# A delta-rule attention with two feed-forward layers: the first group's triangular inverses made in 16x16 blocks and joined on TensorE

## The chip, the cores and the metric

The kernel runs on one core of a Trainium2 chip. Its time is device microseconds of one execution. Three runs of the kernel before gave 926.7, 926.9 and 919.13 us (median 926.7). Engines: PE is TensorE, DVE is VectorE, ACT is ScalarE, POOL is GpSimd, SP is SyncE, whose queue issues every DMA of this kernel in one order.

## The reference

Four batches with eight heads, 768 positions and a head size of 48 go through a delta rule with a state S per head; the result, 3072 tokens of 384 features, goes through two feed-forward layers:

```python
k_n = k / (norm(k) + 1e-6)
for t in range(768):
    y[t] = q[t] @ S
    S = S + beta[t] * outer(k_n[t], v[t] - k_n[t] @ S)
x = y as [3072, 384]
h = x @ w_in;  solu = h * softmax(h);  x = layer_norm(solu) * g_ln @ w_out   # 384 -> 1024 -> 384
g = relu(x @ w2_in) ** 2;  out = g @ w2_out                                  # 384 -> 2048 -> 384
```

The weights arrive as float64, as pairs of 32-bit words.

## The kernel before, in words

**Chunks.** The recurrence is done in chunks of 64 tokens. A step is one chunk of one batch with all eight heads: 4 batches by 12 chunks are 48 steps, and two steps are a tile, 24 tiles in all. Inside a chunk the recurrence needs the inverse of a unit lower triangular 64x64 matrix I + L, with L the lower part of diag(beta) K K^T diag(1/norms). A step multiplies that inverse into the values (zstep, matmul line L1098, result z), then the chain uses z with the state (L1139 to L1182). Steps of one batch follow one another; a step's chain cannot start before its z.

**Inverses.** They are made for groups of tiles: group 0 is tiles 0 to 3, group 1 tiles 4 to 6, group 2 tiles 7 to 10, and four more. For a tile, e_tile multiplies K with K and with Q on PE (L684) out of operands that DVE spreads out by head first (L663), masks the products on DVE (L718), and sends the K K^T part to memory (gscr). norms and gammas work out 1/norm and beta/norm^2 per token in many ops of 24 or 32 elements on DVE. inversion reads gscr back as 32x32 blocks, one in each partition for many blocks at once (tile it), scales them (L881), does a forward substitution in 30 column steps of a multiply (L900) and an add (L917), each of which is split in two on the large steps, and scales again (L942). For group 0 this is on DVE, for groups 1 to 6 on POOL. ACT makes a transposed copy (ia, L959). Both go to memory (tscr, uscr); prep reads them back for one tile (tbd, t2) and joins two 32x32 blocks to a 64x64 one with two sets of 32x32 matmuls on PE (mm1 L1037, mm2 L1050) and copies on ACT (L1057, L1068).

**After that.** moe1_front (18 matmuls of 512 columns, L1218), moe1_back, and moe1_out (72 matmuls for a pair of tiles, L1340) do the first layer, beside the later steps of the recurrence. The second layer (L1483 and L1527) starts when the first has ended. load_w brings a weight piece in: the raw words by DMA into one of two buffers, an Abs on ACT, four DVE ops on 512 or 384 elements, then a high half (a cast on ACT) and a low half (a subtraction, split, L433); for the first layer's 14 pieces the low half is on POOL.

**What sets the order.** Every operation is recorded with an engine, a cost, a priority and what it reads and writes. A planner (class Plan) lays them out in a list schedule by those costs, in twelve rounds, and the kernel is then issued in that order by hand, so each engine and SP's queue run their instructions in a fixed order. The table of priorities (PR) is the same before and after.

## Time and profile before

| | |
|---|---|
| median of the runs | 926.7 us |
| profiled execution: span | 924.3 us (the page gives no other time of this execution) |
| instructions | 23182 |
| PE busy | 862.9 us, 93% of the span |
| DVE, ACT, POOL busy | 515.9, 487.0, 359.7 us |
| first z of tile 0 | at 72.46 us |
| first z of tile 4 (the first of group 1) | at 144.08 us |
| first z of tile 7 (the first of group 2) | at 206.95 us |
| second layer | from 504 us to the end |

Times in a row are microseconds from the start of the span. "PEld" is the loading of weights into PE. A line like L900 is a line of the kernel before; the release in square brackets names what ended an engine's idle time. PEclk is the granted clock of TensorE as a part of its full 2.4 GHz, averaged over the stretch. Rows of SP show the time in which its queue issues, not the transfer.

### The profile page before, as it was taken

The numbers are of one execution on the slowest core, as the hardware profiler recorded it, in microseconds if no ns is written. First come the engines' busy times: TensorE is split into PE (matmuls) and PEld (weight loads), VectorE is DVE, ScalarE is ACT, GpSimd is POOL, SyncE is SP. The second block draws the span as 40 slices with busy tenths as digits, with TensorE's granted clock in tenths as the row PEclk, the third lists the DMA queues.
The fourth block names the chain that finished last, engine by engine and source line by source line (L and its number), as shares of the span: only waits on it lengthen the run. The fifth ranks groups of instructions, "written<-read, shape, count | busy, mean of one in ns | idle before, by whom it ended". The sixth has DMA issues, their size and how long they took to land.

```text
span 924.3 us, 23182 instructions
## 1 busy us (share of the span) xinstructions
PE 862.9 (93%) x9144; PEld 806.9 (87%) x9144; DVE 515.9 (56%) x1063; ACT 487.0 (53%) x1069; POOL 359.7 (39%) x898
## 2 busy tenths in 40 slices
PE   6448888999999999999999999999999999999998
PEld 6447767988887888888788999999999999999998
DVE  6996777623877686766645655343333434343332
ACT  5336689766767667556565645343333434343333
POOL 6399889995468868998300000000000000000000
PEclk8565799999998999999899999999999999999999
DMA  8826967634778676463604432010010101000000
GB/s 238 207 99 157 246 185 210 157 109 113 200 241 251 176 224 179 139 195 114 190 24 144 127 98 77 10 43 10 1 52 1 52 1 52 1 26 1 27 1 26
DMA packets 129244, 101.75 MB, mean 110 GB/s; under 512 B 84080, under 2 KB 106608, under 8 KB 129136
## 3 DMA queue, kind: packets, MB, share of 16 engines
q1 hardware_dynamic: 129136, 100.28, 38.0%
q8 instruction: 72, 1.18, 0.5%
q14 instruction: 36, 0.29, 0.1%
HBM read 70.88 MB, written 29.36 MB: 108 GB/s over the span
## 4 chain that ended last, share of the span: by engine, by line
PE 75%; DVE 8%; DMA 6%; ACT 4%; POOL 3%; issue 2%; SPq 2%; ACTq 0%; DVEq 0%
PE acc L1527 22%; PE h L1483 22%; PE p_h L1218 9%; PE p_x L1340 9%; PE p_z L1098 3%; DMA kqe<-in_kine_dram 2%; PE p_tr L1320 2%; PE p_ep L684 2%; DVE itmp L900 2%; SPq L300 2%; DVE it L917 1%; PE p_a L1139 1%; PE p_o L1155 1%; POOL itmp L900 1%; POOL it L917 1%
## 5 line engine op out<-in xcount | busy, mean ns | idle before, releaser
L1504 DVE TENSOR_TENSOR xt<-xt 128x384 f32<-128x384 f32 x128 | 71.5, 558 | 165.3 <-ACT xt L1496 165.1
L1496 ACT ACTIVATE xt<-h 128x384 f32<-128x384 f32 x128 | 63.0, 492 | 170.7 <-PE h L1483 168.9
L1483 PE MATMUL h<-x1h,w2h 128*128 128x384 f32 x384 | 128.7, 335 | 0.0
L1483 PE MATMUL h<-x1l,w2h 128*128 128x384 f32 x384 | 128.6, 335 | 0.0
L1483 PE MATMUL h<-x1h,w2l 128*128 128x384 f32 x384 | 128.3, 334 | 0.0
L917 POOL TENSOR_TENSOR it<-it,itmp 128x72 f32<-128x72 f32 (+37 forms) x255 | 109.6, 444 | 5.2
L900 POOL TENSOR_TENSOR itmp<-it 128x72 f32<-128x72 f32 (+37 forms) x255 | 107.4, 436 | 2.2
L1340 PE MATMUL p_x<-zh,wgh 128*128 128x256 f32 x288 | 86.9, 302 | 1.3 <-ACT xo L1354 1.1
L1527 PE MATMUL acc<-woh,xl 128*128 128x384 f32 x258 | 87.4, 339 | 0.0
L1527 PE MATMUL acc<-wol,xh 128*128 128x384 f32 x258 | 87.3, 338 | 0.0
L1527 PE MATMUL acc<-woh,xh 128*128 128x384 f32 x258 | 87.0, 337 | 0.0
L1340 PE MATMUL p_x<-zl,wgh 128*128 128x256 f32 x288 | 81.7, 284 | 0.0
L1340 PE MATMUL p_x<-zh,wgl 128*128 128x256 f32 x288 | 81.5, 283 | 0.0
L433 DVE TENSOR_TENSOR xl<-xt,xh 128x384 fp32r<-128x384 f32 x86 | 48.0, 558 | 43.4 <-ACT xh L428 42.9
L1483 PEld LDWEIGHTS h<-x1h,w2l 128*128 128x128 f32 x384 | 72.1, 188 | 0.0
L1483 PEld LDWEIGHTS h<-x1h,w2h 128*128 128x128 f32 x384 | 72.1, 188 | 0.0
L1483 PEld LDWEIGHTS h<-x1l,w2h 128*128 128x128 f32 x384 | 72.1, 188 | 0.0
L428 ACT CAST xh<-xt 128x384 fp32r<-128x384 f32 x86 | 44.2, 514 | 46.1 <-DVE xt L1504 44.8
L1218 PE MATMUL p_h<-w1h,xh 128*128 128x512 f32 x144 | 65.4, 454 | 3.1 <-DVE ez L1251 3.1
L1098 PE MATMUL p_z<-m,tbd 128*128 128x112 f32 x384 | 58.1, 298 | 2.6 <-ACT zs L1109 1.4
L1218 PE MATMUL p_h<-w1h,xl 128*128 128x512 f32 x144 | 59.9, 416 | 0.2 <-DVE xl L433 0.2
L1218 PE MATMUL p_h<-w1l,xh 128*128 128x512 f32 x144 | 59.8, 415 | 0.0
(197 smaller groups left out, 2143.3 us busy)
## 6 DMA issues: line engine op xcount, KB each, us to landing
kql<-in_kin_dram SPq DMA_DIRECT2D x24, 512.0 KB
kqe<-in_kine_dram SPq DMA_DIRECT2D x40, 192.0 KB
raw<-in_w2i_dram SPq DMA_DIRECT2D x12, 512.0 KB
raw<-in_w2o_dram SPq DMA_DIRECT2D x16, 384.0 KB
gscr<-g SPq DMA_DIRECT2D x21, 256.0 KB
m<-in_ktok_dram SPq DMA_DIRECT2D x24, 192.0 KB
vt<-in_vtok_dram SPq DMA_DIRECT2D x24, 192.0 KB
x1scr<-xo SPq DMA_DIRECT2D x12, 384.0 KB
```

The costliest lines, as they stand in the source:

```text
L300: return add("sp", 0.06, lambda: nc.sync.dma_start(dst(), src()), r, w, prio, size, gate)
L428: add("act", c_act(n), lambda: act.copy(hi(), src()), r, [w[0]], prio)
L433: lambda: le.tensor_tensor(out=lo(), in0=src(), in1=hi().bitcast(F32), op=ALU.subtract),
L900: lambda tm=tm, j=j, nr=nr, w_=w_, c0=c0, c1=c1: eng.tensor_tensor(out=tm, in0=it[:, j + 1 :, j : j + 1].to_broadcast([P, nr, w_]), in1=it ...
L917: lambda tm=tm, j=j, c0=c0, c1=c1: eng.tensor_tensor(out=it[:, j + 1 :, c0:c1], in0=it[:, j + 1 :, c0:c1], in1=tm, op=ALU.add,),
L1098: pe.matmul(zp[:, p].rearrange("q (j c) -> q j c", j=7), tb[:, i * NP + p], m[:, i, :, p], start=True, stop=True,)
L1218: pe.matmul(p_h[:, sl], xx[:, c], ww[:, c, sl], start=(c == 0 and k == 0), stop=(c == 2 and k == 2),)
L1340: pe.matmul(p_x1[:, 0 : 2 * P], ww[:, f, c * P : c * P + P], zz[:, f], start=(f == 0 and k == 0), stop=(f == 7 and k == 2),)
L1483: pe.matmul(late["h2", ih], late[ww][:, c, s], xx[:, c], start=(c == 0 and k == 0), stop=(c == 2 and k == 2),)
L1496: lambda: act.activation(out=rt, in_=late["h2", ih], func=AF.Relu),
L1504: lambda: v.tensor_tensor(out=gg, in0=rt, in1=rt, op=ALU.mult),
L1527: pe.matmul(late["acc", a], gg[:, a * P : a * P + P], late[ww][:, f], start=(f == 0 and k == 0), stop=(f == 15 and k == 2),)
```

## The change

It makes group 0's inverses in another way and changes what stands around them.

- **first_group** (new) loads the keys of tiles 0 to 3 ahead of all else, in eight halves of 96 KB, and multiplies 32x32 blocks of K K^T on PE straight into one bank pair (p_h, 128 matmuls). DVE transposes the 32x32 squares of that (1024 elements a partition); each partition then has one row of every block, and the norms are on the diagonal. The scale factors take 17 DVE ops. The substitution runs in 16x16 blocks, two in a partition: 14 steps of a multiply and an add, of at most 112 elements. A scaling and two more transposes give the inverses of the diagonal blocks (d0) and their transposes (u0).
- **combine** (new) joins 16 to 32 (mma, mmb) and 32 to 64 (mm1, mm2) for each of tiles 0 to 3 on PE, 112 matmuls of 32 or fewer columns a tile, with copies on ACT and DVE between; **prep_first** (new) places the results in tbd, by ACT and DVE copies for tile 0 and by six DMAs inside SBUF for tiles 1 to 3. Group 0 no longer uses gscr, tscr and uscr.
- The products with Q of tiles 0 to 3 (**qk_first**) come later, from their own load. The values of a step are scaled on POOL.
- e_tile for tiles 4 to 9 multiplies 64-row operands straight from the loaded keys (eight matmuls of 128 columns for a step, where it was four of 96 rows) without the DVE ops that spread them by head. Their masks are all on DVE, the squares of norms on ACT.
- The first layer's weights: the pieces 3 and 4 use two more raw buffers, their first two DVE ops have one tensor input in place of two, and the 14 subtractions for the low halves go from POOL to DVE. All six w_in pieces are loaded in one go.
- Group 1's inverse on POOL uses another buffer for its products. gammas transposes on DVE in place of PE and ACT. The 20 warming matmuls are gone. The work for tiles 10 to 12 is issued two tiles later.

The core of the diff, in the order of the file:

```diff
-    raw, wu = raw_[i][:, 0:n], w.bitcast(U32)
+    raws, wu = raw_[i], w.bitcast(U32)
+    if n_w[0] in (3, 4):
+        x, kr = ((iaw[:, 0 : HB * HB], [("A", "ia")]), (ez_[0], [("ez", 0)]))[i]
+        raws = x.rearrange("q (n t) -> q n t", t=2).bitcast(U32)
+    raw = raws[:, 0:n]
...
+    if alone:
+        fns = (
+            lambda: v.tensor_scalar(out=w, in0=w, scalar1=F64_LO, scalar2=F64_HI, op0=ALU.max, op1=ALU.min),
+            lambda: v.tensor_scalar(
+                out=wu,
+                in0=wu,
+                scalar1=3,
+                scalar2=0x3FFFFFF8,
+                op0=ALU.logical_shift_left,
+                op1=ALU.bitwise_and,
+            ),
+        )
...
+    for i, fn in enumerate(fns):
+        add("dve", c_dve(n, alone), fn, [], [kw], prio, after=() if i else [*first_inv, *w2_gate])
...
 def load_w1i(i0, i1, prio):
     for i in range(i0, i1):
-        c, n = divmod(i, 2)
+        n, c = divmod(i, 3)
         s = slice(n * 512, n * 512 + 512)
-        w, kw = load_w(w1i[c, :, s], 512, prio)
+        w, kw = load_w(w1i[c, :, s], 512, prio, True)
         split(
             lambda c=c, s=s: w1h[:, c, s],
             lambda c=c, s=s: w1l[:, c, s],
...
-            "pool",
...
+            )[st % 4]
+            gp = bank.rearrange("q (p c) -> q p c", p=NP)
+            kq = kqe_[st % 3].rearrange("q p c -> q (p c)").rearrange("q (a p c) -> q a p c", a=2, p=NP)
+            kkq = [("A", "kqe", st % 3)]
+            dma(lambda kq=kq: kq, lambda st=st: kin[:, st], (), kkq, prio - 1, P * 2048)
+            def mm(gp=gp, kq=kq):
+                for p in range(NP):
+                    for h in range(2):
+                        pe.matmul(
+                            gp[rows[h], p].rearrange("q (a c) -> q a c", a=2),
+                            kq[heads[h], 1, p],
+                            kq[heads[h], :, p],
+                            start=True,
+                            stop=True,
+                        )
+            add("pe", 0.88, mm, kkq, kep, prio)
...
-    add("pe", 0.22, mm, [kbe], [("A", "z")], prio)
-    add("act", c_act(HB), lambda: act.copy(gm, gt), [("A", "z")], [kgm], prio)
+    dv(lambda: v.transpose(out=gm, in_=be), [kbe], [kgm])
...
+def qk_first(t, prio):
+    bank, kbk = ((p_ep, ("A", "ep")), (p_a, ("A", "a")), (p_o, ("A", "o")), (p_z, ("A", "z")))[t]
+    qk = bank.rearrange("q (i p c) -> q i p c", i=2, p=NP)
+    kq, kkq = kq0[t], [("kq0", t, 0), *(("kq0", t, 1, h) for h in range(2)), *keys0[t]]
+    def mm():
+        for j in range(2):
+            for p in range(NP):
+                for h in range(2):
+                    f = heads[h]
+                    pe.matmul(qk[rows[h], j, p], kq[f, j, 1, p], kq[f, j, 0, p], start=True, stop=True)
...
+def first_group(prio):
...
+    for t in range(T1):
+        for h in range(2):
+            f = heads[h]
+            dma(
+                lambda t=t, f=f: kq0[t][f, :, 1],
+                lambda t=t, f=f: kin[f, 2 * t : 2 * t + 2, 1],
+                (),
+                [("kq0", t, 1, h), *([] if h else keys0[t])],
+                prio - 20 + 0.1 * t,
+                D * 2048,
+            )
+    dma(lambda: b, lambda: betag, (), [kb], prio - 18, P * 128)
...
+        def mm_d(kt=kt, t=t):
+            for j in range(2):
+                for p in range(NP):
+                    for e in range(2):
+                        for h in range(2):
+                            k = kt[heads[h], j, p, e * HB : e * HB + HB]
+                            o = (2 * h + e) * HB
+                            pe.matmul(gd[o : o + HB, (2 * t + j) * NP + p], k, k, start=True, stop=True)
+        add("pe", 0.55, mm_d, kk, [kgd[t // 2]], prio + 0.01 * t)
...
+    dv(
+        lambda: v.transpose(out=iaw[:, 0 : HB * HB], in_=gd.rearrange("q s c -> q c s")),
+        kgd,
+        kx,
+        HB * HB,
+    )
...
+    for j in range(1, 15):
+        nr = 15 - j
+        tm = tmb[:, 0 : 2 * nr * j].rearrange("q (b r c) -> q b r c", b=2, c=j)
+        dv(
+            lambda tm=tm, j=j, nr=nr: v.tensor_tensor(
+                out=tm,
+                in0=it16[:, :, j + 1 :, j : j + 1].to_broadcast([P, 2, nr, j]),
+                in1=it16[:, :, j : j + 1, 0:j].to_broadcast([P, 2, nr, j]),
+                op=ALU.mult,
+            ),
+            kit,
+            ktm,
+            2 * nr * j,
+        )
+        dv(
+            lambda tm=tm, j=j: v.tensor_tensor(
+                out=it16[:, :, j + 1 :, 0:j], in0=it16[:, :, j + 1 :, 0:j], in1=tm, op=ALU.add
+            ),
+            ktm,
+            kit,
+            2 * nr * j,
+        )
...
+    first_inv.append(
+        dv(
+            lambda: v.tensor_tensor(out=pd[:, :, :, 0:16], in0=it16, in1=gmr, op=ALU.mult),
+            [*kit, ("A", "it16d"), *kgr],
+            kitp,
+            512,
+        )
+    )
+    _, kd, _, ku = inv_sb(0)
+    dv(
+        lambda: v.transpose(out=d0.rearrange("q s c -> q c s"), in_=full.rearrange("q r c -> q c r")),
+        kitp,
+        [*(("A", "d", t) for t in range(T1)), *kd],
+        HB * HB,
+    )
+    first_inv[0] = dv(
+        lambda: v.transpose(out=u0.rearrange("q s r -> q r s"), in_=itp[:, 0 : HB * HB]),
+        kitp,
+        [*(("A", "u", t) for t in range(T1)), *ku],
+        HB * HB,
...
+def combine(t, prio):
...
+    def mma():
+        for u in range(GS):
+            for s in quads:
+                pe.matmul(yp[s, u], gz[s, u], D_[s, u, 0:16], start=True, stop=True)
+    def mmb():
+        for u in range(GS):
+            for s in quads:
+                pe.matmul(tp[s, u], U_[s, u], ya[s, u], start=True, stop=True)
+        for u in range(GS):
+            for s in quads[1::2]:
+                pe.matmul(up[s.start : s.start + 16, u], ya[s, u], U_[s, u, 16:HB], start=True, stop=True)
+    def mm1():
+        for u in range(GS):
+            for h in range(2):
+                i, o = quads[2 * h], quads[2 * h + 1]
+                pe.matmul(y2[o, u], g01[i, u], D_[i, u], start=True, stop=True)
+    def mm2():
+        for u in range(GS):
+            for s in quads[1::2]:
+                pe.matmul(t2p[s, u], U_[s, u], ysf[s, u], start=True, stop=True)
...
+    add("pe", 0.5, mma, [*kgz, *kd], [kp], prio)
+    add("act", c_act(128), lambda: act.copy(ya, yp), [kp, *ksm], [kya], prio)
+    add("pe", 0.8, mmb, [kya, *ku, *ksm], [kp], prio)
+    add(
+        "dve",
+        c_dve(128),
+        lambda: v.tensor_tensor(out=D_[:, :, 0:16], in0=D_[:, :, 0:16], in1=tp, op=ALU.add),
+        [kp, *kdb],
+        [("A", "d", t)],
...
+    add("pe", 0.3, mm1, [*kd, *ksm], [kp], prio)
+    for h, (en, fn) in enumerate(two):
+        o = quads[2 * h + 1]
+        add(en, c_act(256), lambda o=o, fn=fn: fn(ysf[o], y2[o]), [kp, *ksm], [kys[h]], prio)
+    add("pe", 0.3, mm2, [*kys, *ku, *ksm], [kp], prio)
+    for h, (en, fn) in enumerate(two):
+        o = quads[2 * h + 1]
+        add(en, c_act(256), lambda o=o, fn=fn: fn(U_[o], t2p[o]), [kp, *kub], [("A", "u", t)], prio)
...
+def prep_first(t, prio):
...
+    for q in range(4):
+        s = slice(q * HB, q * HB + HB)
+        o = slice(s.start - HB, s.start)
+        parts = [(s, D_, [("A", "d", t), *kdb], ktb + (q,))]
+        if q % 2:
+            parts.append((o, U_, [("A", "u", t), *kub], ktb + (4 + q // 2,)))
+        for c, src, r, w in parts:
+            if t == 0:
+                en, fn = (("act", act.copy), ("dve", v.tensor_copy))[q // 2]
+                cost = 0.31 if en == "act" else c_dve(256, True)
+                add(en, cost, lambda s=s, c=c, src=src, fn=fn: fn(tb[s, :, c], src[s]), r, [w], prio)
+            else:
+                dma(lambda s=s, c=c: tb[s, :, c], lambda s=s, src=src: src[s], r, [w], prio, HB * 1024)
...
+first_group(-70)
 for t in range(T1):
-    wr = e_tile(t, -70 + t)
-    norms(t, -62)
-gammas(0, -61)
-inversion(0, "dve", -55)
-first_inv.append(plan.writer["A", "it", 0, 0])
+    qk_first(t, -50 + t)
+    ktok_first(t, -45 + t)
+prep(0, PR["prep0"])
+zstep(0, PR["prep0"] + 1)
+load_w1i(0, 6, PR["w1i"])
 for t in range(T1, T2):
     e_tile(t, PR["e0"] + 0.1 * t)
     norms(t, PR["n1"])
 gammas(1, -56)
-warm(5, -55)
-gate.append(wr)
 inversion(1, "pool", PR["inv1"])
-load_w1i(0, 2, PR["w1i"])
 for t in range(T2, LA):
...
-            norms(t + LA, t + PR["norms"])
+        for x in range(0 if t == T1 - 2 else t, t + 1):
+            if T1 - 2 <= t < NT - LA:
+                e_tile(x + LA, x + PR["e"])
+                norms(x + LA, x + PR["norms"])
```

The order that comes of it, at the two places on which the prediction rests. First SP's queue, the loads and stores around group 0's inverse before (tscr and uscr are the memory for the inverses, tbd and t_0 are tile 0's blocks, gscr_77 belongs to tiles of group 2, raw to the weights):

```order
L300 DMA it_213<-gscr_76 24x32x32 x4
...
L300 DMA gscr_77<-g_188 128x512
L300 DMA tscr_82<-it_212 128x1024
L300 DMA uscr_89<-ia 128x1024
L300 DMA tbd_198<-tscr_82 32x8x32 x4
L300 DMA t_0_200<-uscr_89 32x4x32 x4
```

and in the change (be_215 takes beta of a later group; kqe are the keys and queries of a step of tiles 4 and later; gscr_76 and it_212 are the memory and the blocks of group 1; tbd_195<-d_209 is tile 1's placement inside SBUF):

```order
L301 DMA be_215<-in_betat_dram 128x32
L301 DMA kqe<-in_kin_dram 128x512 x2
L301 DMA gscr_76<-g 128x512
L301 DMA kqe<-in_kin_dram 128x512
L301 DMA gscr_76<-g 128x512
L301 DMA g_0_198<-gscr_76 32x8x32 x2
L301 DMA raw_220<-in_w1i_dram 128x1024
L301 DMA kqe<-in_kin_dram 128x512
L301 DMA it_212<-gscr_76 24x32x32 x4
L301 DMA g_1_199<-gscr_76 32x8x32
L301 DMA tbd_195<-d_209 32x8x32
L301 DMA kqe<-in_kin_dram 128x512
```

Tile 0's trip through memory is gone; what now stands in the queue up to tile 0's z are the loads of later tiles and group 1's trip. The first of these rows waits for a DVE op (its buffer be_215 held group 1's factors before), each kqe row for PE.

Then PE up to tile 0's z, before (the warming matmuls, the join of tile 0's blocks, z):

```order
L821 MATMUL p_o<-ident 128x128 x20
L1037 MATMUL p_ep<-tbd_198,g_0_202 32x32 x8
L1037 MATMUL p_a<-tbd_198,g_0_202 32x32 x8
L1050 MATMUL p_ep<-ys,t_0_200 32x32 x8
L1050 MATMUL p_a<-ys,t_0_200 32x32 x8
L1098 MATMUL p_z<-m_172,tbd_198 128x112 x4
```

and in the change, the last rows (L1231 is mma, L1236 and L1239 mmb, L1245 mm1, L1250 mm2, here of tiles 0 to 3 in turn; L696 is the product of K with K and Q for a step of tiles 4 and later):

```order
L1250 MATMUL p_ep<-xt_154,kbd 32x32 x16
L1245 MATMUL p_x_229<-d_209,xt_155 32x32 x16
L1231 MATMUL p_ep<-d_209,xo 32x16 x32
L696 MATMUL p_ab<-kqe 64x128 x8
L1250 MATMUL p_x_229<-xt_155,kbd 32x32 x16
L1236 MATMUL p_ep<-xt_156,kbd 32x16 x32
L1239 MATMUL p_ep<-kbd,xt_156 16x16 x16
L696 MATMUL p_tr<-kqe 64x128 x8
L1231 MATMUL p_x_229<-d_209,xo 32x16 x32
L1422 MATMUL p_z<-m_172,tbd_194 128x112 x4
```

Tile 0's own join ends with the first of these rows; joins of tiles 1 to 3 and two products of later tiles stand between it and z. Further on PE has issued 60 matmuls into p_h and 12 into p_x of the first layer ahead of tile 4's first z before, and 72 and 72 in the change; the other work between the two z is the same to within eight small matmuls.

## Rows read from the trace of the kernel before

**Rows 1.** The page's costliest groups: busy us and mean ns of one, idle before.

```profile
L1340 PE MATMUL p_x<-zh,wgh 128*128 128x256 f32 x288 | 86.9, 302 | 1.3 <-ACT xo L1354 1.1
...
L1218 PE MATMUL p_h<-w1h,xl 128*128 128x512 f32 x144 | 59.9, 416 | 0.2 <-DVE xl L433 0.2
```

**Rows 2.** Windows: length, each engine's busy time (instructions), PEclk, DMA share, GB/s.

```profile
0.00:72.46 72.46, 38.09 (x281) 36.40 (x281) 62.04 (x201) 30.71 (x78) 47.16 (x86) 0.68 0.67 177
72.46:144.08 71.62, 62.87 (x1000) 53.04 (x1001) 51.73 (x103) 51.51 (x123) 63.09 (x144) 0.80 0.75 197
144.08:206.95 62.87, 59.02 (x863) 51.55 (x862) 33.95 (x74) 46.40 (x108) 59.62 (x168) 0.97 0.59 161
206.95:504.00 297.05, 286.32 (x4582) 249.78 (x4581) 198.12 (x391) 193.27 (x437) 189.85 (x503) 0.97 0.58 169
504.00:924.30 420.30, 416.61 (x2425) 416.08 (x2423) 170.06 (x298) 165.11 (x325) 0.00 (x0) 1.00 0.11 34
```

**Rows 3.** The chain of waits in the first 145 us: start, length, engine, what.

```profile
27.64 4.35 DMA gscr<-g
...
62.04 1.55 DVE it L942
```

**Rows 4.** PE's timeline: start, length, instructions, idle time before and its releaser.

```profile
69.01 0.62 PE L1037 MATMUL p_ep<-tbd,g 32*32 32x32 f32 x13 [10.83 <-DMA tbd<-tscr]
...
72.46 2.07 PE L1098 MATMUL p_z<-m,tbd 128*128 128x112 f32 x8 [0.29 <-ACT tbd L1068]
74.45 0.65 PE L1037 MATMUL p_ep<-tbd,g 32*32 32x32 f32 x32
```

**Rows 5.** Group 0's substitution on DVE: minimum/median/maximum ns, first and last start.

```profile
L900 DVE TENSOR_TENSOR itmp<-it x51: 165/280/2441, 33.3 to 60.0; 128x72 f32<-128x72 f32 x3, 128x117 f32<-128x117 f32 x3, 128x21 f32<-128x21 f32 x2, 128x108 f32<-128x108 f32 x2
```

**Rows 6.** DVE's timeline, single instructions.

```profile
8.44 0.42 DVE L663 TENSOR_TENSOR kbd<-kql,hm 96x256 f32<-96x256 f32 x1 [0.51 <-DMA kql<-in_kine_dram]
...
33.76 0.22 DVE L900 TENSOR_TENSOR itmp<-it 128x58 f32<-128x58 f32 x1
34.01 0.22 DVE L917 TENSOR_TENSOR it<-it,itmp 128x58 f32<-128x58 f32 x1
...
48.48 2.60 DVE L900 TENSOR_TENSOR itmp<-it 128x90 f32<-128x90 f32 x2
...
84.33 0.68 DVE L485 SCALAR_TENSOR_TENSOR wst<-wst,cst 128x512 uint32<-128x512 uint32 x1
...
91.25 0.34 DVE L755 TENSOR_REDUCE nrm<-sq 128x4 f32<-128x192 f32 x1
91.52 0.41 DVE L718 TENSOR_TENSOR m<-p_ep,mask 128x256 f32<-128x256 f32 x1
...
113.18 1.21 DVE L1233 TENSOR_REDUCE sc<-p_h 128x1 f32<-128x1024 f32 x1
```

**Rows 7.** ACT's timeline, the transposed copy.

```profile
63.62 1.97 ACT L959 COPY ia<-it 128x1024 f32<-128x1024 f32 x1 [1.77 <-DVE it L942]
```

**Rows 8.** POOL's timeline: group 1's first and last op, others.

```profile
43.76 7.18 POOL L881 TENSOR_TENSOR it<-it,gm 128x1024 f32<-128x1024 f32 x1 [8.21 <-DMA it<-gscr]
...
62.59 1.43 POOL L917 TENSOR_TENSOR it<-it,junk 128x189 f32<-128x189 f32 x1
...
70.36 1.26 POOL L433 TENSOR_TENSOR w1l<-wst,w1h 128x512 fp32r<-128x512 f32 x1
...
114.06 2.35 POOL L881 TENSOR_TENSOR it<-it,gm 128x1024 f32<-128x1024 f32 x1
...
122.39 1.92 POOL L942 TENSOR_TENSOR it<-it,gm 128x1024 f32<-128x1024 f32 x1
```

**Rows 9.** SP's timeline: the time its queue issues.

```profile
0.80 1.34 SPq L300 DMA_DIRECT2D kqe<-in_kine_dram  x3
...
33.73 6.86 SPq L300 DMA_DIRECT2D it<-gscr  x4
...
66.24 2.07 SPq L300 DMA_DIRECT2D tbd<-tscr  x4
```

More of the change, by code (lines that the diff above doesn't have):

```diff
@@ L612, in half @@
         return tile_[:, i * 512 : i * 512 + 512].rearrange("q (p c) -> q p c", p=NP)
+    heads = [slice(h * C, h * C + D) for h in range(2)]
+    rows = [slice(h * C, h * C + C) for h in range(2)]
     def e_tile(t, prio):
@@ new lines, in mm2 @@
+        def mm2():
+            for u in us:
+                for h in range(2):
+                    q = (2 * h + u % 2) * HB
+                    s = slice(q, q + HB)
+                    pe.matmul(tp[s, u // 2], t2[s, u // 2], ys[s, u // 2], start=True, stop=True)
+        r = [*(kg12 + (h,) for h in range(2)), *(ktb + (k,) for k in range(4))]
+        r += [ktb + (4 + h,) for h in range(2)]
+        add("pe", 0.48, mm1, r, [kp], prio)
+        add("act", c_act(128), lambda: act.copy(ys, yp), [kp], kys, prio)
@@ L1106, in zstep @@
         r = [("A", "tbd", t % 2, k) for k in range(4)]
-        r += [("A", "tbd", t % 2, 4 + h, i) for h in range(2)]
+        r += [("A", "tbd", t % 2, 4 + h) for h in range(2)]
         add("pe", 0.86, mm, [*r, ("A", "mp", t % LA, i), ("A", "mk", t % LA)], [("A", "z")], prio)
```

587 lines of the change are left out of this document (351 added, 236 removed).

## The prediction, made before the change was run

> **What bounds the kernel now.** I read the windows first, cut at the first z of tile 0, of tile 4 and of tile 7 and at the start of the second layer [rows 2]. The reader is to see two different kernels in one. Up to 72.46 us PE is busy for 38.09 us; that leaves 34.4 us in which it has nothing to do, at a granted clock of 0.68, while DVE is busy for 62.04. From there on PE is busy 88%, 94%, 96% and 99% of each stretch. So the end is set by PE's work, and by the moment at which PE may start on it. A start that is n us earlier is worth n us, as long as nothing else holds PE back later.
>
> What holds the start is the chain of waits [rows 3]: the store of the products of group 0 (4.35 us), their load, DVE's substitution from 33.3 us on (51 multiplies, the last at 60.0, each with its add, [rows 5]), the scaling at 62.04, ACT's transposed copy [rows 7], the trip to memory and back on SP's queue [rows 9], at which PE has waited 10.83 us when the join begins at 69.01, and z at 72.46 [rows 4].
>
> The second candidate is POOL, which makes group 1's inverse from 43.76 to 122.39 + 1.92 = 124.3 us [rows 8]. Tile 4's z follows it at 144.08. An earlier start that finds group 1 where it was would be lost again.
>
> **The change, part by part: the way to tile 0's z.**
>
> *Keys.* SP issues a load every 1.34/3 = 0.45 us from 0.80 us [rows 9]. The sixth load of 192 KB was in use at 8.44 us [rows 6]. Now it is eight of 96 KB, two thirds of those bytes: 5.6 us if bytes decide, 8.4 at most. I take 7.0. The last 32 blocks on PE cost 0.65 us (32 matmuls of 32x32 in [rows 4]): 7.7.
>
> *DVE up to the inverses.* No row shows the 32x32 transposes of 1024 elements; the nearest are a reduction of 1024 elements out of the same bank in 1.21 us [rows 6] and the two-input scaling of 1024 in 1.55 [rows 3]; I take 1.2, one input: 9.0 with the wait. A small dependent op costs 0.25 from start to start (33.76 to 34.01 in [rows 6]); 17 of them for the factors: 13.2. Then, by the order, 28 substitution ops at 0.25 (7.0; they have at most 112 elements, fewer than most of those they replace), two ops of 512 elements at 0.68 (1.4), 17 small ops of group 1's factors that are threaded between them (4.2), six reductions at 0.34 (2.0), three masks at 0.41 (1.2) and 0.6 for the rest [rows 6]: 16.4, to 29.6. Two more transposes: 32.0.
>
> *DVE up to tile 0's last copy.* 31 rows: 13 ops of 512 elements for the weights, ten masks (4.1), eight others (about 2.4), and the rest of the reductions. Seven of the 13 are of a known form (0.68 each, 4.8); the six with one tensor input have no row: 0.68 bounds them from above and 0.25, a small op, from below, and I take 0.35, since one stream of data is read in place of two (2.1). Sum 13.4: the last copy is at about 45.
>
> *SP's queue.* Tile 0's four trips are gone, but z waits, through PE's order, for a load of keys that stands behind group 1's trip. The queue's first wait in that piece is for DVE's last op of group 1's factors, at about 28.8. Then group 1's last store needs a product whose bank DVE's masks must first free, at about 33.5, and 4.35 us to land [rows 3]: 37.9. The four loads of group 1's blocks took 6.86 us of issue when they had to wait [rows 9], and 1.8 at the bare spacing; I take 5: 42.5. Three more issues (1.4), and 2.8 us to land (tbd was issued at 66.24 and first used at 69.01, [rows 9] and [rows 4]): 46.7. With the last small matmuls, **z at 47 us**; DVE's own way ends at about the same time.
>
> Bounds of that moment: with every price at its lower end 42; with 6.86 for the loads, 4.35 for the landing, and two DVE ops held up by POOL as the one at 48.48 was (2.60 for two ops of some 0.2, [rows 6]) 56.
>
> **PE's work after that moment.** Removed: the joins of tiles 1 to 3, six times 0.65 = 3.9 [rows 4]. Added: 112 small matmuls of joins that are not done by then, 2.3 to 4.5 by the same row, and one product of keys more, eight matmuls of four times 32 columns, about 1.3. Even. The values' scaling on POOL, the squares on ACT and the subtractions on DVE lie beside PE: ACT is busy 72% and DVE 72% of the stretch to 144 [rows 2]; if that cover is gone, tile 4 is late (below).
>
> **The sum.** 72.46 - 47 = 25.5 us earlier: 924.3 - 25.5 = 898.8 us against the profiled execution, whose span is 2.4 us under the median of the runs. **901 us**; 896 to 910 by the bounds of the start alone.
>
> **Does POOL keep up?** Between the two z, PE now does 12 matmuls into p_h and 60 into p_x more: 12 x 0.42 + 60 x 0.30 = 23 us [rows 1]. At the same idle share tile 4's z would be at 144.08 - 25.5 + 23 = 141.6, and 23 us less work would be left behind it. POOL begins group 1 at about 45, as before (43.76). Its 80.5 us lose six low halves at 1.26 (7.6) and the first op of group 2, 2.35, that ran in between, perhaps some of the 4.8 by which its first op is over that (7.18 against 2.35, [rows 8]), and gain four scalings of values of 384 elements, at most the 1.26 of 512 elements each. That is 66 to 75 us: an end at 111 to 120 us, and with the 19.8 us to z as before 131 to 140. Nothing is held up, with 2 to 11 us in hand.
>
> **Rivals.**
>
> *B, more than the start.* The stretch from 72.46 to 144.08 has 8.75 us of PE idle and a granted clock of 0.80 against 0.97 in the next [rows 2]. If the first-layer work moved into it fills the idle time, T is 898.8 - 8.75 + 2.4 = 892; with some of the clock too, 62.87 x (1 - 0.80/0.97) = 11 us, down to 884. For it: that work is plentiful and needs no inverse. Against it: z0 comes early, out of matmuls of a few columns, and the first window's clock with such work was 0.68.
>
> *A, POOL a little late.* DVE now has the subtractions and POOL's ops stretch where DVE's are long: 1.43 us for 189 elements at 62.59, beside DVE's scaling of 1024 elements [rows 8] [rows 3]. If group 1 ends at 125 to 135, tile 4's z is at 145 to 155, 3 to 13 us late: 904 to 914 us.
>
> *C, slower than before: DVE and POOL shut each other out.* The op that POOL started at 43.76 ended at 50.94, and DVE's op of 48.48 ended at 51.1 after 2.60 us [rows 6] [rows 8]: POOL seems to have stood for 4.7 us behind DVE's stream, and DVE then for one whole POOL op. If that is so of every pair, POOL's 66 to 75 us and DVE's busy time in that stretch, some 50 us [rows 2], add up: an end at 161 to 170 and tile 4's z, 19.8 later, at 181 to 190. T is 898.8 + 2.4 + (185 - 141.6) = 945. It turns slower when tile 4's z is later than 167. Against it: the stretch before had both engines busy for 51.73 and 63.09 of 71.62 us [rows 2], which is more than the stretch holds if they take turns. The Trainium skill's page "SBUF — State Buffer", section "Who interferes with whom", states this rule: an instruction of VectorE with two inputs in SBUF, or a one-input copy or tensor_scalar in its two-port mode, and one of GpSimd hold the shared ports in turn, whole instructions at a time. Where the rule holds, the change's new one-input ops would be among those that shut POOL out, and C would be the result; the two rows agree with it, the sum of the busy times does not.
>
> *D, the start is not what it says.* The trips for group 0 are gone, but z hangs on SP's queue, which has DVE, PE and ACT in series in front of it. If each of its waits costs a few us more, z is at 57 to 66: 911 to 920.
>
> **Chances.** The forecast (895 to 910) 0.52; B (884 to 895) 0.20; A beyond that (to 914) 0.10; D 0.11; C 0.07. The range from 886 to 915 leaves out the end of B, most of D and C, some 2 in 10. A measurement of this kernel tells about 1% from no change, 917.4 to 936: faster 0.87 (all of the forecast, A and B, half of D), same 0.07, slower 0.06.
>
> **What would show it.** Right: the first z between 42 and 56 us; DVE's substitution ended by 30; group 1's last POOL op before 122; PE idle before tile 4's z under 3 us on a release by the inverse. Wrong: a first z that SP's queue released after 56; z of tile 4 waiting for a DMA of group 1's inverse for over 5 us; POOL's substitution ops of about 190 elements at 1.43 us or more, as at 62.59 [rows 8], beside DVE ops of 512; a granted clock in the first stretch that falls to half for long, so that the joins take twice 0.65 for 32.

## The result, and the profile after

The change makes the kernel slower by half a per cent: 1.0051 of the time before, interval 1.0027 to 1.0074, medians 929.3 and 925.8 us of 20 runs each. Forecast were 901 us, a range of 886 to 915, and a chance of 0.87 for faster. The profiled execution has a span of 929.3 us, against 924.3. Executions of one kernel differ with the mean clock that TensorE was granted: the changed kernel's 20 lie between 922.5 us at 0.963 and 934.1 us at 0.940, so a difference of some us between two profiled executions is not the edit's alone.

The windows of the changed kernel, cut at the same events as [rows 2]: the first z of tile 0 and of tile 4, then a point in the second layer at which the rest takes as long as before. The columns are those of [rows 2]; in this kernel z is line L1422 and POOL's inverse L885 to L943.

```profile
0.00:63.20 63.20, 46.38 (x1360) 42.55 (x1360) 39.83 (x131) 21.33 (x55) 19.30 (x47) 0.73 0.68 201
63.20:150.90 87.70, 76.29 (x1123) 66.11 (x1117) 59.55 (x130) 62.04 (x139) 65.69 (x170) 0.79 0.54 144
150.90:509.00 358.10, 337.11 (x5340) 293.49 (x5340) 222.77 (x452) 226.81 (x517) 240.02 (x655) 0.96 0.58 164
509.00:929.30 420.30, 416.83 (x2419) 415.22 (x2418) 168.45 (x295) 163.95 (x322) 0.00 (x0) 1.00 0.10 33
```

Read them as length minus PE's busy time. Idle time of PE before the first z went from 34.4 to 16.8 us, so the start did gain 17.6. Between the two z it is 11.4 us (8.8 before), from there to the last cut 21.0 (14.6 before): 9 us given back. And PE is busy for 876.6 us in all, 13.7 more than before (862.9). 17.6 - 9.0 + 0.2 (the last stretch) - 13.7 = -5.0, which is the difference of the spans. The first z is at 63.2 us, 9.3 earlier than before and 16 later than forecast; tile 4's z is at 150.9, 6.8 later than before.

Where the 13.7 us are: PE's groups of the joins, by line, with busy us and mean ns (the last two rows are the old join, now for 20 tiles).

```profile
L1236 PE MATMUL p_x<-xt,kbd 32*32 32x16 f32 x128 | 2.7, 211 | 0.1
...
L1245 PE MATMUL p_ep<-d,xt 32*32 32x32 f32 x64 | 2.1, 237 | 0.0
...
L1231 PE MATMUL p_x<-d,g 32*32 32x16 f32 x64 | 1.3, 210 | 0.6 <-issue 0.6
...
L1391 PE MATMUL p_ep<-ys,t 32*32 32x32 f32 x640 | 9.5, 198 | 3.8 <-ACT ys L1396 3.8
L1378 PE MATMUL p_ep<-tbd,g 32*32 32x32 f32 x640 | 9.1, 194 | 2.4 <-DMA tbd<-tscr 1.4 <-DVE m L743 0.9
```

All twelve groups of the new joins (two or four of each kind) are 20.6 us for four tiles, the old one 18.6 us for twenty. Every matmul of these joins and of the key products leaves two records in the trace: the order's x16 is x32 in a row, and the 112 matmuls of a tile are 224 records. The records are 211 and 237 ns long, but they overlap, so what one costs is the busy time over the count: 16 to 21 ns at 16 columns on 32 rows, 33 ns at 32 columns. Before, all joins were 24.2 us; the new sum of 39.2 is 15.0 more. The products of keys, with keys and with queries, in smaller pieces up to tile 9, add 7.1, and the warming matmuls and small transpositions that went save 6.9. (Groups overlap a little, so these do not add up to 13.7 exactly.)

These are busy times, and the granted clock is in them. By the trace's records of the clock, 70.1 us of PE's busy time were at 0.50 before and 80.7 are now. The first such record comes at 9.4 us before and at 22.8 us now; up to there a window prints 1.00 without a reading (so the 0.68 of [rows 2] and the 0.73 above are too high), and PE is busy for 5.2 and 17.1 us of that time. Its pace there is that of half clock: 32 records of L696 took 3.62 us at 18.62, 16 took 1.09 at 26.29, when a record says 1.00, and 1.97 at 38.21 at 0.50 (rows below). An estimate from these figures, which counts each us of both kinds as half a us, puts the whole of PE's work at 825.3 us of full clock before and 827.7 now. So about 2.4 of the 13.7 us are added work; the rest is that more of the work was done at half clock, where the change put it.

PE's timeline up to the first z, with the idle time before a row and what ended it:

```profile
10.03 1.92 PE L1059 MATMUL p_tr<-kql 48*64 48x32 f32 x32
...
18.62 3.62 PE L696 MATMUL p_h<-kqe 48*64 48x128 f32 x32
...
26.29 1.09 PE L696 MATMUL p_h<-kqe 48*64 48x128 f32 x16
...
38.21 1.97 PE L696 MATMUL p_ab<-kqe 48*64 48x128 f32 x16 [7.74 <-DVE m L979]
40.11 1.05 PE L1231 MATMUL p_ep<-d,g 32*32 32x16 f32 x64
...
44.06 1.97 PE L696 MATMUL p_h<-kqe 48*64 48x128 f32 x16
45.97 1.36 PE L1236 MATMUL p_x<-xt,kbd 32*32 32x16 f32 x63
...
60.32 1.97 PE L696 MATMUL p_tr<-kqe 48*64 48x128 f32 x16
62.23 1.05 PE L1231 MATMUL p_x<-d,xo 32*32 32x16 f32 x64
63.20 2.05 PE L1422 MATMUL p_z<-m,tbd 128*128 128x112 f32 x8
```

From 38.2 us on there is hardly a gap: six products of later tiles at 1.9 us each, and 336 of the 448 matmuls of the joins between them, all at half clock. The window of that stretch says so (PE busy 23.29 of 24.99 us, granted clock 0.50). The clock had fallen at 29.7 us, by its records, and did not rise before 87.7, although PE was busy nearly all of the time from 38.2 on:

```profile
38.21:63.20 24.99, 23.29 (x768) 20.68 (x768) 18.41 (x41) 11.76 (x30) 9.23 (x17) 0.50 0.57 145
```

DVE's timeline, the three transposes, and the wait in the substitution:

```profile
10.17 1.25 DVE L1086 STREAM_TRANSPOSE iaw<-p_h 128x1024 f32<-128x1024 f32 x1 [9.03 <-PE p_h L1048]
...
16.61 0.16 DVE L1162 TENSOR_TENSOR it<-it 128x28 f32<-128x28 f32 x1
...
23.04 0.42 DVE L743 TENSOR_TENSOR m<-p_h,mask 128x256 f32<-128x256 f32 x1 [6.27 <-ACT g L732]
...
33.86 1.93 DVE L1199 STREAM_TRANSPOSE kbd<-itp 128x1024 f32<-128x1024 f32 x1
35.65 1.91 DVE L1193 STREAM_TRANSPOSE d<-itp 128x1024 f32<-128x1024 f32 x1
```

A mask of tile 4 stands behind the second op of the substitution, and waits 6.27 us: the product that it masks is one PE does after group 0's (the row at 18.62). The inverses are ready at 37.6 us.

POOL's timeline, group 1's first op, two scalings of values (L1315), and the last op, with SP's rows behind them in a second fence (SP's times are those of issue):

```profile
53.09 2.35 POOL L885 TENSOR_TENSOR it<-it,gm 128x1024 f32<-128x1024 f32 x1 [25.53 <-DMA it<-gscr]
...
81.76 0.99 POOL L1315 TENSOR_TENSOR vt<-vt,nrm 128x384 f32<-128x384 f32 x1 [14.55 <-DMA vt<-in_vtok_dram]
...
96.34 0.83 POOL L1315 TENSOR_TENSOR vt<-vt,nrm 128x384 f32<-128x384 f32 x1 [5.55 <-DMA vt<-in_vtok_dram]
...
134.64 1.92 POOL L943 TENSOR_TENSOR it<-it,gm 128x1024 f32<-128x1024 f32 x1
```

```profile
27.79 5.76 SPq L301 DMA_DIRECT2D be<-in_betat_dram  x2
...
72.46 2.56 SPq L301 DMA_DIRECT2D tbd<-d  x4
...
76.24 1.16 SPq L301 DMA_DIRECT2D vt<-in_vtok_dram  x1
```

Group 1's inverse starts 9.3 us later than before [rows 8], after a queue that stood 5.8 us for DVE, and lasts 83.5 us instead of 80.5, although six subtractions left POOL: it stands 20.1 us for values. Its ops themselves were not slower: those of the substitution took 48.6 us in all, 50.5 before. (Values were scaled on POOL before as well; what is new is their place in its order.) Their load is behind four DMAs that place tile 2's inverse (tbd), which wait until tile 0's second z has read that buffer.

### The profile page after: what moved, and what is told of

Its sections match the earlier page's. It is cut to its first block, busy times and chain, and to the rows that moved or that the text cites. A ratio compares the mean times of both kernels' runs of the same rounds, so it can differ in the third digit from the quotient of the medians.

```text
span 929.3 us, 25174 instructions
## 1 busy us (share of the span) xinstructions
PE 876.6 (94%) x10232; PEld 817.4 (88%) x10232; DVE 490.6 (53%) x1007; ACT 474.1 (51%) x1033; POOL 325.0 (35%) x870
## 4 chain that ended last, share of the span: by engine, by line
PE 79%; DVE 8%; ACT 5%; DMA 4%; issue 3%; SPq 2%; ACTq 0%; DVEq 0%
PE acc L1855 22%; PE h L1811 21%; PE p_x L1668 9%; PE p_h L1546 8%; PE p_z L1422 4%; PE p_ab L1467 2%; PE p_tr L1648 2%; PE p_ep L726 2%; SPq L301 2%; DMA raw<-in_w2i_dram 1%; PE p_ab L1483 1%; PE p_ab L1482 1%; DVE wst L539 1%; ACT xt L1516 1%; PE p_tr L1535 1%
## 5 line engine op out<-in xcount | busy, mean ns | idle before, releaser
L918 POOL TENSOR_TENSOR it<-it,itmp 128x57 f32<-128x57 f32 (+37 forms) x306 | 131.0, 444 | 6.5
L903 POOL TENSOR_TENSOR itmp<-it 128x57 f32<-128x57 f32 (+37 forms) x306 | 131.2, 444 | 2.6
L1422 PE MATMUL p_z<-m,tbd 128*128 128x112 f32 x384 | 59.0, 302 | 0.6 <-ACT zs L1433 0.6
```

What stands on the lines that cost most here:

```text
L903: lambda tm=tm, j=j, nr=nr, w_=w_, c0=c0, c1=c1: eng.tensor_tensor(out=tm, in0=it[:, j + 1 :, j : j + 1].to_broadcast([P, nr, w_]), in1=it ...
L918: lambda tm=tm, j=j, c0=c0, c1=c1: eng.tensor_tensor(out=it[:, j + 1 :, c0:c1], in0=it[:, j + 1 :, c0:c1], in1=tm, op=ALU.add,),
L1422: pe.matmul(zp[:, p].rearrange("q (j c) -> q j c", j=7), tb[:, i * NP + p], m[:, i, :, p], start=True, stop=True,)
```

## The experiments

Two theories to begin with. **W**: PE's own work, 13.7 us more of busy time and over half of it ahead of the first z, took the gain. **P**: POOL's waits inside group 1's inverse made tile 4's z late, and that took it. Each ratio is to the kernel before, run on the same chip; the changed kernel's is 1.0051. Where the edit leaves the planner's input as it was, the order is the same; else the planner lays out the whole program anew.

### Scaling of two tiles on DVE

```diff
-        add("pool", c_pool(384, False), lambda: pool.tensor_tensor(out=vt, ...
+        en, eng = ("dve", v) if t in (2, 3) else ("pool", pool)
+        add(en, ..., lambda: eng.tensor_tensor(out=vt, ...
```

> The changed kernel, but the scaling of tile 2's and 3's values runs on DVE instead of POOL. Theory P (in the changed kernel POOL stood 14.6 + 5.6 us in the middle of group 1's inverse for these two loads, so tile 4's z came at 150.9 us and the gain of the start was lost): the inverse ends at 116 to 122 us instead of 136.6, tile 4's z comes 8 to 13 us earlier, the time falls by 6 to 12 us. Theory W (PE's own work, 13.7 us more than before, takes the gain; waits are a symptom): POOL's inverse is earlier but the time falls by 0 to 3 us.

1.0050 [1.0018, 1.0083]. POOL waits as long as before, now at tile 4's scaling, so the run tells nothing of P:

```profile
POOL vt L1316 <- DMA vt<-in_vtok_dram: 17.1, 1, 17.1
```

### A quarter of the 16-to-32 joins, same order

```diff
-            for u in range(GS):   # in mma and mmb
+            for u in range(2):
```

> The changed kernel in the same order, but the 16-to-32 joins of tiles 0 to 3 issue a quarter of their matmuls (80 of 320), which leaves most off-diagonal 16x16 blocks of group 0's inverses out: some 9 us less busy time on PE, nearly all of it around tile 0's z at half clock. Theory W: the first z comes 5 to 7 us earlier and the time falls by 6 to 10 us. Theory P: the first z comes earlier, tile 4's z stays where POOL puts it, and the time falls by 0 to 4 us (what POOL's waits follow from the earlier chain).

0.9956 [0.9923, 0.9988], 9 us under the changed kernel. PE's busy time is 867.3 instead of 876.6; the first z is at 55.6 instead of 63.2, tile 4's at 141.6 instead of 150.9. W's numbers; but POOL's waits for values had also shrunk, from 21.0 to 8.9 us, so P was not out yet. By the estimate above, at full clock, the cut took only 3.4 us off (824.3 against 827.7): these matmuls are dear because they run at half clock.

### Later tiles' products behind the first z

```diff
-                add("pe", 0.88, mm, kkq, kep, prio)
+                add("pe", 0.88, mm, kkq, kep, prio, after=z_first if t >= T2 else ())
```

> The changed kernel, but the products of keys of tiles 7 to 9 may only follow tile 0's first z on PE: five steps of 1.9 us and some joins move behind it. If the place of the first z decides (theory S): z at 50 to 54 us instead of 63.2, time 6 to 10 us lower. Theory W: the work is only moved, time within 2 us. Theory P: the chain of tile 0 frees the value buffer earlier, POOL's wait of 14.6 us shrinks by the same 9 us, time 3 to 6 us lower.

1.0031 [0.9999, 1.0063]. The first z came 6.9 us earlier, tile 4's 3.4, the time 0.2% lower. The place of the first z alone brought little: what was moved behind it still has to be done. (The order is another one here; see the draws below.)

### The weights' part undone

```diff
-            w, kw = load_w(w1i[c, :, s], 512, prio, True)
+            w, kw = load_w(w1i[c, :, s], 512, prio)
             split(...
+                "pool",
-        if n_w[0] in (3, 4):
+        if False:
```

> The changed kernel with one part undone: the first layer's weights are converted as before (two-input ops on DVE, low halves on POOL, two raw buffers). Theory P: POOL has 14 more ops (14 us) beside group 1's and 2's inverses, the waits stay: 0 to 6 us slower. Theory W: PE's work is the same: within 2 us. If the new one-input ops on DVE shut POOL out (rival C of the prediction): POOL's substitution ops get shorter and the time falls by 3 us or more.

1.0190 [1.0153, 1.0226], 1.4% slower than the changed kernel. Tile 4's z is at 164.1: POOL now waits for ACT's casts of the weights, 19.5 us in all up to there. This edit undoes three things at once, and the order is another one. Rival C, DVE shutting POOL out, would have made this run faster. POOL's 105 substitution ops of group 1 did take less, 45.5 us against 48.6; that is 3 us, where C needed tens, and the time went the other way.

### Scaling of five tiles on DVE

```diff
+        en, eng = ("dve", v) if 2 <= t < T2 else ("pool", pool)
-            prio - (60 if t >= T1 else 0),
+            prio - (60 if t >= T2 else 0),
```

> The changed kernel, but the scaling of the values of tiles 2 to 6 runs on DVE; in the run before this one (tiles 2 and 3 only) POOL's wait had merely moved to tile 4's scaling (17.1 us). Now nothing of POOL's work between the first and last op of group 1's inverse waits for a load of values. Theory P: the inverse takes 62 to 68 us instead of 83.5 and ends at 115 to 124, tile 4's z comes at 131 to 141 instead of 150.9, the time falls by 6 to 12 us. Theory W (PE's own work and the time at which it starts set the end): the inverse ends as early, PE's idle time before tile 4's z (11.4 us from the first z) falls by some us at most: time 0 to 4 us lower.

0.9957 [0.9932, 0.9982], faster than both kernels. But not as P has it: POOL waits 13.4 us for group 2's factors instead, its last op of group 1 ends at 133.8, and tile 4's z is at 150.9, where it was. The time is gained after it.

### The substitution ahead of all else on DVE

```diff
+                after=sub_done if t < LA else (),   # masks of tiles 4 to 9, reductions
```

> The changed kernel, but on DVE the masks and reductions of tiles 4 and later may only follow group 0's substitution, so that its second op no longer stands 6.3 us behind a mask that waits for PE. Theory W: the inverses are ready at 27 to 30 us instead of 37.5, PE's idle stretch of 7.7 us before its joins is filled, the first z comes at 54 to 58, the time falls by 5 to 8 us. Theory P: group 1's factors come later (by 3 to 6 us), POOL starts and ends later, the time is within 3 us or higher, though the first z is earlier.

1.0065 [1.0034, 1.0096]. The inverses are ready at 30.8 us, 6.8 earlier, and the first z comes at 62.6: 0.6 earlier. PE has three waits before it now that nothing in the profile explains ("issue", 3.6, 1.8 and 1.7 us), and the same work. The time that W forecast was missed too.

### Warming matmuls in PE's idle stretch

```diff
+            if j > 6:
+                add("pe", 0.45, warm, [], [("x1",)], prio, after=[len(plan.ops) - 1])   # 4 of 128x128
```

> The changed kernel with 32 matmuls of 128x128 more on PE, put in while it waits for group 0's substitution (it was idle from 30.5 to 38.2 us, and the granted clock in the joins after it was 0.50). If the clock is what makes the joins and products before the first z long (25 us, theory W with the clock as its cause): 1.0 in part of the stretch from 38 to 63, first z at 52 to 58, time 4 to 9 us lower. If the clock falls again with these small matmuls whatever ran before: no change or up to 4 us slower, by what the added matmuls take.

1.0127 [1.0092, 1.0162]. The first z is at 71.1. In this run the clock was 1.00 from 21 to 38 us, where PE was busy 4.61 of the last 8 us, and 0.50 in the joins behind it. So the clock fell again, although it had been up to then; the loss, some 7 us against the changed kernel, is more than was expected. No run here kept the clock at 1.00 through the joins, so what they would cost there stays an estimate:

```profile
30.00:38.00 8.00, 4.61 (x53) 3.89 (x51) 8.00 (x34) 1.20 (x3) 0.87 (x1) 1.00 0.19 50
38.00:50.00 12.00, 8.12 (x348) 7.62 (x350) 6.90 (x18) 2.80 (x11) 0.00 (x0) 0.50 0.42 108
```

### The weights' part alone, on the kernel before

```diff
+        w, kw = load_w(w1i[c, :, s], 512, prio, True)   # one-input ops
-                "pool",                                 # low halves on DVE
```

> The kernel before with one part of the change alone: the first layer's weights are converted with one-input ops and the low halves made on DVE instead of POOL. In the changed kernel, undoing this part cost 9.6 us more (939 against 929). If that gain belongs to the part: the kernel before falls by 5 to 10 us. If it is a gain only in the changed kernel, since there all six pieces stand beside group 1's inverse: within 3 us. If rival C of the prediction holds (DVE shuts POOL out): slower by 2 us or more, since DVE is busy 62 of 72 us before the first z.

1.0025 [0.9992, 1.0058]: no change clear of noise. The order is new here too, and new orders of the kernel before with no other change were 0.6 and 0.9% slower (below), so whether the part itself gains something is not shown.

### POOL's waits for values removed, same order

```diff
+            x = it_[0].rearrange("q r c -> q (r c)")[:, (t - 2) * 384 : (t - 1) * 384]   # tiles 2, 3
+        order.remove(load_v[k]); order[order.index(load_v[i])] = load_v[k]   # 4, 5 for 2, 3
+        order[j:j] = load_v[2:4]   # behind the loads of group 1's blocks
```

> The changed kernel in the same order on every engine, but the values of tiles 2 and 3 go to places of their own (in a buffer that is idle then) and their loads stand right behind those of group 1's blocks on SP's queue; tile 4's and 5's loads take the old places of these two. So POOL's two waits (14.6 and 5.6 us) inside group 1's inverse go, and nothing else moves. Theory P: the inverse ends at 115 to 119 us instead of 136.6, tile 4's z comes as early as PE's work lets it (about 140), time 6 to 10 us lower. Theory W: PE has 10 us of idle time between tile 2's z and tile 4's; at most 3 of them go, time within 3 us.

1.0015 [0.9985, 1.0045]. In this kernel group 2's blocks were loaded over tile 3's values before its chain had read all of them, so tile 3's results are others (its chain waited 2.0 us for that load). The waits for values are gone, and another took their place:

```profile
POOL it L886 <- DVE gm L828: 19.3, 1, 19.3
```

The order has group 2's first op ahead of group 1's last ones, and DVE had not made group 2's factors yet.

### The planner's costs as measured

```diff
-            add("pe", 0.45, mm_g, ...      -        add("pe", 0.6, mm, kkq, [kbk], prio)
+            add("pe", 0.9, mm_g, ...       +        add("pe", 0.95, mm, kkq, [kbk], prio)
```

> The changed kernel, but the planner is told what the trace showed for the new operations: the 64x32 products 0.9 instead of 0.45 of its units, Q's products 0.95 instead of 0.6, the products of tiles 4 to 9 0.95 instead of 0.88, the last two joins 0.42 instead of 0.3, and the two last transposes 1.9 us instead of 1.1. Theory M (the order is bad because these costs were too low: a mask in front of the substitution, values too early on POOL): first z 3 to 8 us earlier, POOL's waits under 10 us, time 4 to 9 us lower. Theory W: another order of the same work, within 4 us either way.

1.0051 [1.0021, 1.0082]. First z 65.4, tile 4's 148.7. Theory M falls.

### Two other draws of the order

```diff
-            add("pe", 0.55, mm_d, ...
+            add("pe", 0.56, mm_d, ...
```

> The changed kernel, with one cost that the planner knows changed by 2% (0.55 to 0.56 for the 32 matmuls of one tile's 32x32 blocks): no work differs, but the order does all along. It tells what another order alone does to the time. If the order carries little: within 2 us. If the experiments that make the planner run anew are as much another draw as another design: 4 us or more either way.

1.0012 [0.9981, 1.0043], 0.4% under the changed kernel with the same work.

> The kernel with the scaling of tiles 2 to 6 on DVE (9 us faster than the changed kernel), with the same 2% in the planner's one cost. If its gain comes from POOL having no wait for values: it stays, 6 to 10 us under the changed kernel. If it came from a lucky order: it falls to 0 to 4 us.

1.0034 [1.0005, 1.0062], against 0.9957 in the first draw. The fast version was a lucky order.

### No wait on POOL, same order

```diff
+            x = itp[:, (t - 2) * 384 : (t - 1) * 384]   # tiles 2, 3; the loads moved as above
+        early = [i for i in order[: pos[end]] if i in inv_ops[2] and plan.ops[i][0] == "pool"]
+        order = [i for i in order if i not in early]
+        order[n:n] = early                              # group 2 behind group 1 on POOL
```

> The changed kernel in its own order, with the values of tiles 2 and 3 in places of their own (a buffer that nothing uses any more) and loaded early, and with group 2's operations on POOL moved behind the last of group 1's: when only the values were early, POOL waited 19.3 us for group 2's factors instead. Theory P: group 1's inverse now takes 60 to 66 us from its start at 53 and ends by 120; tile 4's z comes at 134 to 142 instead of 150.9 and the time falls by 7 to 12 us. Theory W: the inverse ends by 120, tile 4's z stays within 4 us of 147, since PE has that much to do before it in its order; time 3 to 5 us lower, as with the early values alone.

1.0042 [1.0016, 1.0068]. POOL's last op of group 1 ends at 112.5, 24 us earlier. Tile 4's z is at 148.3, 2.6 earlier, and the time has hardly moved. The inverse now lies there until SP's queue, in its order, comes to its store 19 us later:

```profile
110.55 1.92 POOL L944 TENSOR_TENSOR it<-it,gm 128x1024 f32<-128x1024 f32 x1
```

```profile
131.25 0.38 SPq L301 DMA_DIRECT2D tscr<-it  x1
```

PE needs the transposed copy as well. ACT makes it in its own fixed order, at 134.3 us, and its store is issued 2.6 us earlier than in the changed kernel (136.42 against 139.00), which is just what tile 4's z gained:

```profile
136.42 0.32 SPq L301 DMA_DIRECT2D uscr<-iaw  x1
```

PE, meanwhile, is busy for 74.3 of the 85.1 us between the two z. So P falls in part: POOL may be freed of 24 us, and the end does not follow, because the orders of ACT and SP bring the inverse to PE hardly earlier. What an earlier inverse would bring was not tried; it could at most fill PE's 10.8 idle us.

> The same, and the 16-to-32 joins of tiles 0 to 3 issue a quarter of their matmuls (most off-diagonal 16x16 blocks of group 0's inverses are left out). With the joins cut alone the time fell by 9 us, but POOL's waits fell by 12 us too. Theory W: 7 to 10 us below the run without the cut, since PE's busy time falls by that. Theory P: 0 to 4 us below it, since with POOL free the cut has nothing left to shorten.

0.9948 [0.9922, 0.9975], 0.9% under the run without the cut, as in the first pair. PE's busy time fell by 8.5 us and the time by 7 to 9, whatever POOL waited for. That is W, as far as the busy time goes; at full clock, by the estimate above, the cut is worth 3.1 us.

### The kernel before in two other orders

```diff
-        add("pe", 0.86, mm, [*r, ...      -        add("pe", 0.22, mm, [kbe], ...
+        add("pe", 0.87, mm, [*r, ...      +        add("pe", 0.23, mm, [kbe], ...
```

> The kernel before with one of the planner's costs changed by 1% (z's 0.86 to 0.87): no work differs, only the order. If the order of the kernel before is an ordinary draw: within 2 us of it on either side. If it is a well chosen one, and any change that makes the planner run anew loses that: 3 to 8 us slower.

1.0086 [1.0056, 1.0117].

> The kernel before with another of the planner's costs changed (the transposition of group factors, 0.22 to 0.23). Same question, a second draw: within 2 us if the order is ordinary, 3 to 8 us slower if it is a chosen one.

1.0063 [1.0030, 1.0095]. Both slower with the same work: PE's busy time is 862.2 and 856.1 us, not more than before, its idle time 71.1 and 67.8 against 61.4. The kernel before sits in a better order than these two.

Busy time, too, depends on the draw and on the execution. The first run with another order above has the same matmuls as the changed kernel, and PE is busy 12.6 us less in its profile (the changed kernel first):

```profile
PE 876.6 (94%) x10232; PEld 817.4 (88%) x10232; DVE 490.6 (53%) x1007; ACT 474.1 (51%) x1033; POOL 325.0 (35%) x870
```

```profile
PE 864.0 (94%) x10232; PEld 806.8 (88%) x10232; DVE 489.2 (53%) x1007; ACT 473.1 (52%) x1033; POOL 325.4 (35%) x870
```

By the clock's records it has 52.9 us of busy time at 0.50, against 80.7. Over the changed kernel and the three runs that do its matmuls in new orders (both other draws, the costs as measured), PE is busy 864.0 to 876.6 us and idle 52.1 to 54.1; over the kernel before and its two draws, busy 856.1 to 862.9 and idle 61.4 to 71.1. At full clock, by the estimate, all seven lie between 825.3 and 829.2. That is what holds over the draws: less idle time, more busy time, nearly the same work.

## Why the prediction was wrong

**The keys** are in place when forecast (the last load of them had landed at 6.5 us, forecast 7.0); the last of the first products runs to 10.1 us (forecast 7.7), held 2.0 us by nothing that the profile shows. **DVE up to the inverses**: 37.6 us against 32.0. The transpose out of the bank came out as priced (1.25 against 1.2, a guess from the nearest rows), the two others were priced too low (1.9 each against 1.2), and the order's mask between two ops of the substitution costs 6.3. That is a miss of 5.6 us, but not the one that mattered: with the inverses at 30.8 us the first z stayed at 62.6.

**"With the last small matmuls, z at 47 us"** is the step that failed. The order printed ahead of the prediction shows PE's rows before z, among them two products and the joins of three tiles, and I priced the queue of SP and the chain of DVE through all of them but PE's as a remainder. By rows that were at hand, 1.9 us for a product (of the old form) and 0.65 for 32 records of a join, which are 16 matmuls, both at a granted clock of 0.50, the stretch is six products and 336 matmuls: 11.4 + 13.7 = 25 us. It took 25.0 and put z at 63.2. The row of a product and the clock at the old join, in the kernel before:

```profile
22.39 1.92 PE L684 MATMUL p_ep<-kql,kbd 96*128 96x128 f32 x8
```

```profile
69.00:72.46 3.46, 1.77 (x65) 1.36 (x65) 3.46 (x7) 2.15 (x8) 3.46 (x6) 0.50 0.41 92
```

The prediction also read those 32 records as 32 matmuls, for the keys' blocks and for the lower bound of the joins, which halves the price, and took 0.65 for a price that a half clock would double; it was the price at half clock already. An engine that is idle for 34 us at the start looked like one with room for any number of small matmuls.

**"PE's work after that moment: even"**, and with it "a start that is n us earlier is worth n us", is the second. The sum compared what is left after z in either kernel, and never the whole. The whole is 13.7 us more of busy time, in a kernel where PE is busy 93% of the span. Both cuts of the joins (9.3 and 8.5 us of busy time) gave the time back nearly one for one. Even was nearly right for the work at full clock (2.4 us more, an estimate); what the sum left out is that the idle time it fills at the start lies at half clock, so that the same work takes more of it. The prediction's own sign of being wrong, a granted clock that falls to half for long in the first stretch, came: 0.50 from 29.7 us to beyond z.

**"Does POOL keep up?"** It did not: 136.6 us against 111 to 120. The late start (53.1) and two waits for values are what I had not seen. What this cost stays open: in the run without these waits the inverse reached PE only 2.6 us earlier. The forecast for tile 4's z, 141.6, assumed the same work from a z at 47. Its term of 23 us for the first-layer matmuls moved between the two z was too large: PE's time on them there went from 21.5 to 32.0 us, 10.5 more. The 0.30 us priced for each of the 60 into p_x is the length of a record, and these overlap.

**The rivals.** D was the nearest (z at 57 to 66), with the wrong engine and without PE's added time. A's tile 4 came true (z at 145 to 155, measured 150.9), but by luck: POOL was late for its start and its waits, not for stretched ops. B did not come: between the two z the clock was 0.79 (0.80 before) and PE's idle time 11.4 us (8.8 before). Nor did C: POOL's first op of group 1 took 2.35 us instead of 7.18, its op of 189 elements 0.57 instead of 1.43, and undoing the ops that were to shut it out made the changed kernel slower by 1.4%:

```profile
84.45 0.57 POOL L918 TENSOR_TENSOR it<-it,itmp 128x189 f32<-128x189 f32 x1
```

What the Trainium skill's page "SBUF — State Buffer", section "Who interferes with whom", says of turns at the shared port may hold for a pair of ops, as the rows of [rows 6] and [rows 8] show; it did not decide this time.

**What I left out altogether** is the order. Any edit makes the planner draw another one for the whole program. Four draws of the changed kernel's work or nearly so (it, with costs 2% other, with costs as measured, with later products moved) gave 1.0051, 1.0012, 1.0051 and 1.0031; three of the kernel before gave 1, 1.0086 and 1.0063. So of the half per cent that was measured, the part that belongs to the change cannot be told from that of its draw; against other draws of its own the kernel before would have lost. Three or four draws are too few to say that the change gains, and this stays open. None came near the 2.8% that was forecast.

## What to carry to other kernels

Where one engine is busy for over 90% of the span, sum that engine's busy time over the whole program before and after, first of all, each part at the granted clock of the stretch in which it will run; idle time at the start is no free room for it if what is put there must end before the start can. Take the price of a small matmul from busy time over the count, not from the length of a record, and see how many records a matmul leaves. Where a planner lays out the order, measure two or three draws of both kernels before a difference of half a per cent is put down to an edit.

## What the runs showed of the hardware that was not expected

A 32x32 transpose of 1024 elements a partition took 1.25 us out of a bank and 1.9 us from SBUF to SBUF; the two from SBUF also write with a stride, so which of the two makes the difference is not shown. PE's first products of Q took about twice as long as the last ones of the same form (32 records, 16 matmuls: 1.95 and 1.09 us). A window prints a granted clock of 1.00 for both stretches, but the trace's first record of the clock comes only at 22.8 us, between the two:

```profile
16.88 1.95 PE L1001 MATMUL p_ep<-kql 48*64 48x64 f32 x32
...
23.30 1.09 PE L1001 MATMUL p_ab<-junk 48*64 48x64 f32 x32
```

The joins ran at a granted clock of 0.50 after idle time (the changed kernel, PE busy 23.29 of 24.99 us) and after matmuls of 128x128 at 1.00 (the run with warming matmuls, PE busy 8.12 of 12.00 us in the joins) alike.
